# A row of sums spread over partitions: two DMAs through DRAM in the place of a TensorE matmul (two layers of linear attention and MLP)

## The chip, the cores and the metric

The kernel runs on one core of one Trainium2 chip. The metric is the device time of one execution in microseconds (us), lower is better. The engines are called as in the profile: PE (TensorE), DVE (VectorE), ACT (ScalarE), POOL (GpSimd) and SP (SyncE), which here only issues DMAs. POOL issues the large weight loads between its own operations.

## The reference

```python
def A(x, wqkv, wo):                      # linear attention, H = 32 heads of 16
    q, k, v = split(x @ wqkv)            # per head
    phi = lambda t: where(t > 0, t + 1, exp(t)) + 1e-6
    pq, pk = phi(q), phi(k)
    kv = einsum("bhsd,bhse->bhde", pk, v)
    z = einsum("bhsd->bhd", pk)          # the row of phi(K) sums, 512 numbers
    num = einsum("bhqd,bhde->bhqe", pq, kv)
    den = einsum("bhqd,bhd->bhq", pq, z)[..., None] + 1e-6
    return (num / den) @ wo
def B(x, w1, b1, w2, b2):                # MLP, 512 -> 1792 -> 512
    return gelu(layernorm(x) @ w1 + b1) @ w2 + b2
x = x + A(layernorm(x)); x = x + B(layernorm(x))     # layer one
x = x + A(layernorm(x)); x = x + B(layernorm(x))     # layer two
```

x is [1, 2048, 512]; all inputs and the output are bfloat16. Both layers use the same weights.

## The kernel before

**Tiles.** The 2048 tokens are 16 tiles of 128 (one token to a partition), four tiles to a chunk, so four chunks, 0 to 3. Names end in the layer (0 is layer one, 1 is layer two), then the tile or the chunk, then a part: WO0_8 is layer one, tile 8; Q0_1_2 is layer one, chunk 1, part 2.

**Order.** Nothing is scheduled when it runs. Every operation has a name, and `CONF["ORDER"]` (L345) holds one list of names for each engine, written out in full. A planner (`Scheduler`, L114) steps through these lists with its own costs, hands out buffers and PSUM banks, and `assign_waits` (L283) derives the semaphore waits. On the chip each engine goes through its list strictly in order (`play`, L1306): an operation that waits holds up all that stand behind it. SP's list is the order of its DMA issues. `CONF["WAY"]` says which engine does an operation that can go to two.

**The operations around the change**, in the order of the work:

- stats, aggr (DVE), veps, pow (POOL; pow gives rstd), nmr (POOL), norm (DVE or ACT): a layer norm. normB ends in yb.
- TA, TB, TP (SP): DMA transposes of a 128x512 tile (L793 for TA and TB, L1078 for TP). PT (PE, L806) with tc (ACT, L816) is a transpose by PE instead; PTB0_0 and PTB1_0 are such.
- K (L861), Q (L879 by token, L892 by channel), exp, relu, min, phi: phi of keys and queries. G (L962, L994) sums y by phi(K), KV (L1017) multiplies by wv, kvm masks to the heads, M (L1040) multiplies by wo.
- Z (PE, L943) and zs (DVE, L949, L952): the 512 sums of phi(K), as zs[128, 4], that is with channel k*128+p in partition p, column k. zs0_2 is the last of layer one. zb (L1023) is the same, masked, for the chunks whose denominator PE computes by channel (D, L1086; then ln, rec, pr on ACT and DVE or POOL).
- For the chunks whose denominator is computed by token (chunks 2 and 3 of layer one, 1, 2 and 3 of layer two) the 512 sums are needed as one row, the same in all 128 partitions: **zrow**[128, 512]. dz (DVE, L1028) multiplies the identity by zs, ZR (PE, L1031) multiplies a matrix of ones by dz, and cpz (ACT, L975) copies the bank to zrow.
- pz (phi(Q) times zrow, DVE or POOL, L1062), red, den, rec, pr: the denominator by token. pz0_2_0 is the first reader of zrow in layer one.
- WO (PE, L1110): the attention's output, and RA (DVE, L1115): its residual, which frees WO's bank. Two such banks are held at a time.
- W1 (PE, L1142; W10 in layer one, W11 in layer two) with gelu (ACT, L1148), W2 (PE, L1181; W20 and W21) with RB (DVE): the MLP. W10 of chunk 0 is done in two halves: `W10_0_5_0` reads tiles 0 and 1, `W10_0_5_1` tiles 2 and 3. Each of the 14 groups of a half has four matmuls of 256 columns. b2 adds the bias b2 to x (DVE or POOL, L1127).
- w1_0, w1_1, w2_0, w2_1, wv, wo: loads of the weights, issued by POOL (L683). A reader of w1 or of w2 waits for both halves (`Graph.parts`).

The work of layer one's end of attention and start of MLP lies between 34 and 106 us of the span. WO0_8 is the first WO of chunk 2: it reads what TP0_2_0 has transposed, after pr0_2_0. W20_1_0 is the first reader of w2.

Of the kernel before, what the change touches and what calls it, by code (L numbers as in the profile page):

```python
# [10 lines left out]
P = 128  # L11
S = 2048
D = 512
# [269 lines left out]
def assign_waits(graph, order, sems, dma_sems):  # L283
# [10 lines left out]
    while len(done) < total:  # L294
        moved = False
        for e in ENGINES:
# [247 lines left out]
def build_kernel(nc, A_x, A_wqkv, A_wo, B_x, B_w1, B_b1, B_w2, B_b2, out, conf=None, report=False):  # L544
# [5 lines left out]
    with ExitStack() as es:  # L550
# [37 lines left out]
        eps6 = SB("eps6", [P, 1], FP32)  # L588
        dz = SB("dz", [P, D], BF16)
        zrow = SB("zrow", [P, D], BF16)  # L590
        zacc = SB("zacc", [P, D], FP32)
        rd = SB("rd", [P, 4, H], FP32)
        rr = SB("rr", [P, 4, H], FP32)
        if report:
# [783 lines left out]
```

## Time and profile before

| | |
|---|---|
| median of 3 runs | 325.43 us (325.35 to 325.6) |
| profiled execution | 325.09 us |
| its span | 323.4 us |
| mean granted clock of PE in it | 1.0 |

The profile is that of one execution. Its span runs from the first to the last instruction; the execution's own time is 1.7 us longer. A line of the engines in order of time gives start, length, engine, source line, operation, output<-inputs, shapes and how many were merged (x); the bracket gives the idle time of the engine just before it and what ended it. Busy times of PE include the pipeline behind each matmul, so the distance between two starts says what a matmul costs, not its length. PEld is PE's weight load, which overlaps. Lines of DMA issues give KB and the median us from issue to landing. In the lists of groups by line the first number behind the bar is busy us, the second mean ns of one.

### The profile page before, as it was taken

To read this page: it belongs to the slowest core of one execution; us is meant where nothing else is said; L and a number is where in the kernel's file an instruction comes from. 1 tells how busy PE (TensorE), PEld (TensorE's weight loads), DVE (VectorE), ACT (ScalarE), POOL (GpSimd) and SP (SyncE) were. 2 spreads that over 40 slices of the span, in tenths; PEclk is the share of its full clock that TensorE was granted. 3 is DMA by queue.
4 is the path that set the end of the run, shared out by engine and by line. 5 is a ranking of instruction groups with operands and counts; after the bars stand their busy time and mean duration, and the time that the engine had idled before them with its cause. 6 is when DMAs were issued, how large, how long until landed. Compare 5 with 4: busy or idle time off the path is not lost.

```text
span 323.4 us, 4794 instructions
## 1 busy us (share of the span) xinstructions
PE 319.9 (99%) x1725; PEld 159.1 (49%) x1725; DVE 215.5 (67%) x506; ACT 195.1 (60%) x335; POOL 135.4 (42%) x224
## 2 busy tenths in 40 slices
PE   8999999999999999999999999999999999999996
PEld 4444545675444444444444444458644444444443
DVE  5998769999985660214759999999898664000232
ACT  5999698873136129488974657879913734576000
POOL 4672278638703359000366645873902934000000
PEclk9999999999999999999999999999999999999999
DMA  7514458212320105310003200121252243000004
GB/s 246 175 39 94 146 144 305 60 34 59 72 49 12 39 16 99 67 32 2 0 0 68 49 16 2 23 59 36 50 84 49 49 53 79 16 0 2 32 25 155
DMA packets 47572, 20.52 MB, mean 63 GB/s; under 512 B 42620, under 2 KB 46076, under 8 KB 47548
## 3 DMA queue, kind: packets, MB, share of 16 engines
q1 hardware_dynamic: 46076, 15.19, 20.9%
q0 software_dynamic: 1056, 4.72, 4.6%
q10 hardware_dynamic: 416, 0.30, 0.3%
q8 instruction: 14, 0.23, 0.3%
q14 instruction: 10, 0.08, 0.1%
HBM read 8.00 MB, written 2.10 MB: 31 GB/s over the span
## 4 chain that ended last, share of the span: by engine, by line
PE 92%; DVE 6%; POOL 1%; issue 0%
PE ps L1142 30%; PE ps L1181 29%; PE ps L861 9%; PE ps L1110 7%; PE ps L962 4%; PE ps L892 3%; PE ps L879 3%; PE ps L994 2%; PE ps L699 1%; PE ps L1168 1%; DVE gtb L1007 1%; DVE rd L1065 1%; PE ps L943 1%; DVE xsb L1115 1%; DVE gacc L1004 1%; PE ps L1086 1%
## 5 line engine op out<-in xcount | busy, mean ns | idle before, releaser
L1148 ACT ACTIVATE gT<-ps,b1c 128x512 bf16<-128x512 f32 (+1 forms) x140 | 77.2, 600 | 64.4 <-PE ps L1142 63.5
L1142 PE MATMUL ps<-t,w 128*128 128x512 bf16 (+1 forms) x560 | 101.3, 337 | 0.0
L1181 PE MATMUL ps<-w,gT 128*128 128x512 bf16 x434 | 98.4, 379 | 0.0
L1142 PEld LDWEIGHTS ps<-t,w 128*128 128x128 bf16 x560 | 54.5, 98 | 43.8 <-ACT t L816 0.3
L1181 PEld LDWEIGHTS ps<-w,gT 128*128 128x128 bf16 x434 | 42.3, 98 | 50.2
L758 POOL TENSOR_TENSOR rstd<-veps,neghalf 128x1 f32<-128x1 f32 x64 | 39.3, 627 | 5.0 <-DVE veps L756 2.8
L831 ACT ACTIVATE eb<-ps 128x512 bf16<-128x512 f32 x56 | 32.4, 605 | 11.3 <-PE ps L879 3.7
L1191 DVE TENSOR_TENSOR pkb<-ps,xsb 128x512 bf16<-128x512 f32 x15 | 10.2, 685 | 41.5 <-PE ps L1181 41.5
L743 DVE BATCH_NORM_STATS2 stats<-xsb 128x6 f32<-128x512 f32 x48 | 32.1, 677 | 0.3
L861 PE MATMUL ps<-wqkv,t 128*128 128x512 bf16 x128 | 31.4, 379 | 0.0
L1110 PE MATMUL ps<-gtb,t 128*128 128x512 bf16 x128 | 31.3, 380 | 0.1
L842 ACT ACTIVATE rb<-ps 128x512 bf16<-128x512 f32 x38 | 22.8, 607 | 9.3 <-PE ps L861 7.0
L748 POOL TENSOR_SCALAR veps<-mv 128x1 f32<-128x1 f32 x32 | 9.0, 282 | 42.9 <-DVE mv L745 40.9
L756 POOL TENSOR_SCALAR veps<-mv 128x1 f32<-128x1 f32 x28 | 7.1, 258 | 45.5 <-DVE mv L745 44.1
L778 ACT ACTIVATE yb<-xsb,nmr,rstd 128x512 bf16<-128x512 f32 x21 | 16.7, 812 | 11.4 <-POOL nmr L775 11.4
L783 DVE TENSOR_SCALAR yb<-xsb,mv,rstd 128x512 bf16<-128x512 f32 x27 | 14.9, 560 | 11.9 <-POOL rstd L758 11.6
L1187 DVE TENSOR_TENSOR xsb<-ps,xsb 128x512 f32<-128x512 f32 x16 | 10.9, 682 | 16.8 <-PE ps L1181 16.8
L879 PE MATMUL ps<-wqkv,t 128*128 128x512 bf16 x80 | 20.2, 379 | 0.0
L1110 PEld LDWEIGHTS ps<-gtb,t 128*128 128x128 bf16 x128 | 12.3, 98 | 14.8 <-ACT gtb L975 0.3
L861 PEld LDWEIGHTS ps<-wqkv,t 128*128 128x128 bf16 x128 | 12.3, 98 | 14.8 <-ACT t L816 0.3
L844 DVE TENSOR_SCALAR eb<-eb 128x512 bf16<-128x512 bf16 x46 | 13.8, 312 | 8.2 <-ACT eb L831 8.0
L1127 POOL TENSOR_TENSOR xsb<-xsb,b2b 128x512 f32<-128x512 f32 x14 | 17.1, 1218 | 1.0 <-DVE yb L783 0.7
(103 smaller groups left out, 395.0 us busy)
## 6 DMA issues: line engine op xcount, KB each, us to landing
w<-in_B_w_dram POOLq DMA_DIRECT2D x4, 896.0 KB, 7.5
out_dram<-pkb SPq DMA_DIRECT2D x15, 128.0 KB, 2.0
t<-in_A_x_dram SPq DMA_DIRECT2D x3, 512.0 KB, 6.7
t<-yb SPq DMA_TRANSPOSE x57, 2.5
wqkv<-in_A_wqkv_dram SPq DMA_DIRECT2D x1, 512.0 KB, 5.2
wqkv<-in_A_wqkv_dram POOLq DMA_DIRECT2D x1, 512.0 KB, 4.3
wo<-in_A_wo_dram POOLq DMA_DIRECT2D x1, 512.0 KB, 5.7
t<-t SPq DMA_TRANSPOSE x20, 2.5
```

Of the source, the lines that this page charges most:

```text
L743: G.op("dve", lambda e: e.bn_stats(stats[:, s.slot, :], src()), 602, reads=src_keys, writes=[k + "s"], tiles=[s, *src_tiles], prio=prio, n ...
L758: G.op("pool", lambda e: e.tensor_tensor(rstd[:, s.slot:s.slot + 1], veps[:, s.slot:s.slot + 1], neghalf[:], op=ALU.pow), 530, reads=[k + ...
L778: G.op("act", lambda e: e.activation(yb[:, y.slot, :], src(), ACT.Identity, bias=nmr[:, s.slot:s.slot + 1], scale=rstd[:, s.slot:s.slot + 1]),
L831: G.op("act", lambda e: e.activation(eb[:, et.slot, :], bank(bt), ACT.Exp, scale=factor()), 569 if by else 483, reads=[src_key, *more], wr ...
L842: G.op("act", lambda e: e.activation(rb[:, rt.slot, :], bank(bt), ACT.Relu, scale=factor()), 569 if by else 478, reads=[src_key, *more], w ...
L861: ins = e.matmul(bank(b), lhsT=yTa(yT)[:, dt, k * P:(k + 1) * P], rhs=wqkv[:, dt, D:2 * D], start=(dt == 0), stop=(dt == DT - 1))
L879: ins = e.matmul(bank(b), lhsT=yTa(yT)[:, dt, k * P:(k + 1) * P], rhs=wqkv[:, dt, 0:D], start=(dt == 0), stop=(dt == DT - 1))
L1110: ins = e.matmul(bank(wb), lhsT=yTa(pq)[:, kt, k * P:(k + 1) * P], rhs=gtb[:, kt, :], start=(kt == 0), stop=(kt == DT - 1))
L1127: G.op("pool" if on_pool else "dve", lambda e: e.tensor_tensor(xsb[:, st, :], xsb[:, st, :], b2b[:], op=ALU.add), 1120 if on_pool else 600 ...
L1142: ins = e.matmul(bank(b, n), lhsT=w1[:, dt, ft * P:(ft + 1) * P], rhs=yTa(yT)[:, dt, k0 * P:k1 * P], start=(dt == 0), stop=(dt == DT - 1))
L1148: G.op("act", lambda e, ft=ft, b=b, k0=k0, k1=k1, n=n: e.activation(gT[:, g.slot, ft * 512 + k0 * P:ft * 512 + k1 * P], bank(b, n), ACT.Ge ...
L1181: ins = e.matmul(bank(b), lhsT=gT[:, g.slot, ft * 512 + k * P:ft * 512 + (k + 1) * P], rhs=w2[:, ft, :], start=(ft == 0), stop=(ft == FT - 1))
```

## The change

In layer one zrow is made by two DMAs: zsc0 (DVE) copies zs to bfloat16, ZW0 (SP) writes the 128x4 numbers to a DRAM tensor of 512 in the order of channels, and ZB0 (SP) reads these 512 as one row into all 128 partitions. Layer two keeps dz, ZR and cpz.

```diff
+        zsb = SB("zsb", [P, DT], BF16)
+        zscr = nc.dram_tensor("zscr", [D], BF16, kind="Internal").ap()
...
             if any(by_token(L, c) for c in range(NC)):
-                zr = Tile(psum, f"zr{L}", "t")
...
+                if L == 0:
+                    G.op("dve", lambda e: e.tensor_scalar(zsb[:], zs[:], 1.0, None, op0=ALU.mult), 90, reads=["zs"], writes=["zsb"], prio=prio + 8,
+                         name=f"zsc{L}", lat=40)
+                    dma("sp", lambda e: e.dma_start(zscr.rearrange("(k p) -> p k", p=P), zsb[:], allow_slow_non_contiguous=True), ["zscr"], reads=["zsb"], prio=prio + 8, name=f"ZW{L}", kb=2)
+                    dma("sp", lambda e: e.dma_start(zrow[:], bass.AP(zscr.tensor, zscr.offset, [[0, P], [1, D]])), ["zrow"], reads=["zscr"], prio=prio + 8,
+                        name=f"ZB{L}", kb=128)
+                else:
+                    zr = Tile(psum, f"zr{L}", "t")
...
```

The lines behind `else` are those of before (dz, ZR, cpz; L1027 to L1033), indented.

The lists are new in two places. In layer one, from about Z0_2 to the end of W10 of chunk 0 (the parts that differ, cut):

```diff
 PE
-Z0_1 G0_4_0 Z0_2 Q0_1_2 Q0_1_1 G0_5_0 D0_0_3 D0_0_0 G0_6_0 D0_0_1 G0_7_0 D0_0_2 G0_8_0 ZR0 G0_9_0
+Z0_1 G0_4_0 Q0_1_2 Z0_2 Q0_1_1 G0_5_0 D0_0_0 D0_0_1 G0_6_0 G0_7_0 D0_0_2 D0_0_3 G0_8_0 G0_9_0
...
-WO0_8_0 W10_0_3_1 W10_0_12_1 W20_1_0 W10_0_5_1 W10_0_2_1 W20_1_7
+WO0_8_0 W10_0_12_0 W20_1_0 W10_0_10_1 W10_0_12_1 W20_1_7
 DVE
-zs0_1 minq0_1_3 zs0_2 zb0 phiq0_1_3 phiq0_0_1 dz0 minq0_1_0 minq0_1_2 phiq0_1_0 pr0_0_0 minq0_1_1
+minq0_1_0 phik0_9 phiq0_1_0 zs0_1 zs0_2 zsc0 zb0 minq0_1_3 phiq0_0_1 minq0_1_2 phiq0_1_3 minq0_1_1 pr0_0_0
...
-pz0_2_0 red0_2_0 RA0_0 statsB0_0 RA0_1 statsB0_1 aggrB0_0 aggrB0_1 RA0_2 RA0_3 normB0_1 statsB0_2 normB0_0
+pz0_2_0 red0_2_0 RA0_0 statsB0_0 RA0_1 aggrB0_0 statsB0_1 aggrB0_1 den0_2_0 RA0_3 rec0_2_0 normB0_1 RA0_2 normB0_0
+RA0_6 statsB0_2 RA0_4 statsB0_3 aggrB0_3 statsB0_6 pr0_2_0
 POOL
-phik0_6 w1_1 phiq0_1_2 wv wo w2_1 phiq0_1_1 w1_0 pr0_0_2 pr0_1_0 pr0_1_1 w2_0 pr0_1_2 pr0_1_3
+phik0_6 w1_1 w1_0 phiq0_1_1 wv wo phiq0_1_2 pr0_0_2 pr0_1_0 w2_0 pr0_1_1 pr0_1_2 pr0_1_3
...
-b20_0 vepsB0_2 powB0_2 vepsB0_3 powB0_3 phiq0_2_3 pz0_2_1
+b20_0 w2_1 vepsB0_3 powB0_3 vepsB0_2 powB0_2 phiq0_2_3 vepsB0_4
 SP
-Tb1 TB0_1 TB0_2 TB0_3 TP0_2_0 TB0_5
+Tb1 ZW0 ZB0 TB0_1 TP0_2_0 TB0_3 TB0_2 TB0_5
```

In PE's list before, 19 groups of W10 stood between WO0_7 and WO0_8: the 14 of the first half and 5 of the second. In the new one there are 13, all of the first half. In layer two's first chunk the lists of DVE, ACT, POOL and SP are permuted, PE's is not:

```diff
 DVE
-RA1_0 statsB1_0 RA1_1 aggrB1_0 statsB1_1 den1_1_3 aggrB1_1
+RA1_0 RA1_1 statsB1_0 statsB1_1 den1_1_3 aggrB1_1
...
-pr1_1_3 RA1_2 phiq1_3_0 statsB1_2 normB1_0 aggrB1_2 RA1_5 RA1_3
+pr1_1_3 RA1_2 aggrB1_0 statsB1_2 RA1_5 aggrB1_2 normB1_0 phiq1_3_0 RA1_3
```

More of the change, by code (lines that the diff above doesn't have):

```diff
@@ L1026, in attn_kv @@
             if any(by_token(L, c) for c in range(NC)):
-                zr = Tile(psum, f"zr{L}", "t")
-                G.op("dve", lambda e: e.tensor_tensor(dz[:].rearrange("p (k c) -> p k c", k=DT), idp[:].unsqueeze(1).broadcast_to([P, DT, P]),
-                                                      zs[:].unsqueeze(2).broadcast_to([P, DT, P]), op=ALU.mult), 600,
-                     reads=["zs", f"id{P}"], writes=["dz"], prio=prio + 8, name=f"dz{L}", lat=40, fast=True)
-                G.op("pe", lambda e: e.matmul(bank(zr), lhsT=onesm[:, 0:P], rhs=dz[:], start=True, stop=True), MM,
-                     reads=["dz", "onesm"], writes=[f"zr{L}"], tiles=[zr], prio=prio + 8, name=f"ZR{L}", lat=MM_DRAIN)
-                copy(zrow[:], zr, f"zr{L}", "zrow", True, prio + 8, f"z{L}")
+                if L == 0:
[6 more added lines that the diff above has]
+                    zr = Tile(psum, f"zr{L}", "t")
+                    G.op("dve", lambda e: e.tensor_tensor(dz[:].rearrange("p (k c) -> p k c", k=DT), idp[:].unsqueeze(1).broadcast_to([P, DT, P]),
+                                                          zs[:].unsqueeze(2).broadcast_to([P, DT, P]), op=ALU.mult), 600,
+                         reads=["zs", f"id{P}"], writes=["dz"], prio=prio + 8, name=f"dz{L}", lat=40, fast=True)
+                    G.op("pe", lambda e: e.matmul(bank(zr), lhsT=onesm[:, 0:P], rhs=dz[:], start=True, stop=True), MM,
+                         reads=["dz", "onesm"], writes=[f"zr{L}"], tiles=[zr], prio=prio + 8, name=f"ZR{L}", lat=MM_DRAIN)
+                    copy(zrow[:], zr, f"zr{L}", "zrow", True, prio + 8, f"z{L}")
             for kt in range(DT):
```

164 rows, old and new, of the table ORDER are left out of this document.

## The prediction

> **What bounds the kernel now.** I read the page first, then the busy time by stretches, then the engines in order of time where the change lies.
>
> ```profile
> span 323.4 us, 4794 instructions
> PE 319.9 (99%) x1725; PEld 159.1 (49%) x1725; DVE 215.5 (67%) x506; ACT 195.1 (60%) x335; POOL 135.4 (42%) x224
> ```
>
> ```profile
> core 0: us, PE busy (x) PEld busy (x) DVE busy (x) ACT busy (x) POOL busy (x), PEclk, DMA share, GB/s
> 34.00:62.00 28.00, 28.00 (x180) 14.10 (x178) 23.72 (x55) 22.64 (x41) 18.34 (x21) 1.00 0.58 180
> 62.00:106.00 44.00, 44.00 (x257) 24.72 (x255) 38.88 (x85) 21.54 (x46) 20.03 (x30) 1.00 0.22 46
> ```
>
> The page's first part gives TensorE 319.9 of 323.4 us. In the stretch where the edited code runs (34 to 62 us) it is busy 28.00 of 28.00 us, and in the next one 44.00 of 44.00, at granted clock 1.00. A busy share can hide a slow TensorE, so I look at the distance between starts:
>
> ```profile
> 44.83 0.38 PE L1031 MATMUL ps<-dz,onesm 128*128 128x512 bf16 x1
> 45.05 2.32 PE L962 MATMUL ps<-pkb,yb 128*128 128x512 bf16 x10
> ```
>
> The matmul to be removed starts at 44.83 and the next at 45.05. The row says 0.38 us, but a matmul of 512 columns occupies the engine for 0.22; the other 0.16 is pipeline that the next one overlaps. TensorE is thus the bound from end to end: what leaves it is gained whole, what leaves another engine is gained not at all, and a wait on it, however short, is lost. One wait is there already, in layer two:
>
> ```profile
> 212.09 1.03 PE L1110 MATMUL ps<-gtb,t 128*128 128x512 bf16 x4
> 213.06 0.19 POOL L748 TENSOR_SCALAR veps<-mv 128x1 f32<-128x1 f32 x1
> 213.34 0.55 POOL L758 TENSOR_TENSOR rstd<-veps,neghalf 128x1 f32<-128x1 f32 x1
> 213.92 0.55 DVE L783 TENSOR_SCALAR yb<-xsb,mv,rstd 128x512 bf16<-128x512 f32 x1 [0.47 <-POOL rstd L758]
> 214.47 1.25 DVE L1115 TENSOR_TENSOR xsb<-ps,xsb 128x512 f32<-128x512 f32 x2
> 214.68 0.39 PE L806 MATMUL ps<-idp,yb 128*128 128x128 bf16 x4
> 215.18 1.41 PEld L1110 LDWEIGHTS ps<-gtb,t 128*128 128x128 bf16 x8 [0.30 <-DVE xsb L1115]
> 215.19 1.90 PE L1110 MATMUL ps<-gtb,t 128*128 128x512 bf16 x8
> ```
>
> VectorE waits 0.47 us for GpSimd's rstd at normB1_0 (213.92). Behind it in VectorE's list stands RA1_5, the first of the two at 214.47, and WO1_7 (215.19) needs the bank that RA1_5 frees. The bracket shows the weight load idle 0.30 us for L1115; the four matmuls at 214.68 take 0.39 - 0.16 = 0.23 us, so matmuls could go on at 214.91 and go on at 215.19: 0.28 us lost.
>
> **The change part by part.** *TensorE:* ZR0 goes, -0.22 us. No matmul is added; the rest are permuted.
>
> *ScalarE and VectorE:*
>
> ```profile
> L1028 DVE TENSOR_TENSOR dz<-idp,zs 128x512 bf16<-128x512 bf16 x2 | 1.4, 682 | 0.0
> L975 ACT ACTIVATE zrow<-ps 128x512 bf16<-128x512 f32 x2 | 1.2, 592 | 0.7 <-PE ps L1031 0.7
> L935 DVE TENSOR_SCALAR zs<-ps 128x4 f32<-128x4 f32 x1 | 0.2, 151 | 0.0
> ```
>
> ScalarE loses cpz0, 0.59 us. VectorE loses dz0 (0.68) and gains zsc0, a copy of 128x4 for which L935 is the nearest row, 0.15. Both savings lie beside a TensorE without a gap, so I count them as nothing; they only widen margins.
>
> *The two DMAs.* The trace has no write of 512 two-byte elements. The nearest rows:
>
> ```profile
> t<-yb SPq DMA_TRANSPOSE x57, 2.5
> out_dram<-pkb SPq DMA_DIRECT2D x15, 128.0 KB, 2.0
> t<-in_A_x_dram SPq DMA_DIRECT2D x2, 128.0 KB, 2.6
> b2b<-in_B_b_dram SPq DMA_DIRECT2D x1, 128.0 KB, 3.3
> b1t<-b1r SPq DMA_TRANSPOSE x1, 7.3
> w<-in_B_w_dram POOLq DMA_DIRECT2D x1, 896.0 KB, 7.6
> wqkv<-in_A_wqkv_dram POOLq DMA_DIRECT2D x1, 512.0 KB, 4.3
> wo<-in_A_wo_dram POOLq DMA_DIRECT2D x1, 512.0 KB, 5.7
> w<-in_B_w_dram POOLq DMA_DIRECT2D x1, 896.0 KB, 5.8
> ```
>
> The last number is us from issue to landing. The row of 7.6 is w1_1, issued beside b2b and b1t; the row of 5.8 is w2_0, the last load. b1t moves 4 KB and still took 7.3 us, as long as the load beside it. So ZW0 costs between 2.0 (a store to DRAM) and 7.3 (beside a load), ZB0 between 2.6 and 7.3. When do they start, and beside what?
>
> ```profile
> 35.20 0.94 POOL L683 DMA_DIRECT2D w<-in_B_w_dram  x1
> 38.39 0.54 PE L943 MATMUL ps<-onesm,pkb 128*128 128x1 bf16 x16
> 38.97 0.16 DVE L952 TENSOR_TENSOR zs<-ps,zs 128x4 f32<-128x4 f32 x1 [0.61 <-PE ps L943]
> 52.24 0.68 DVE L1062 TENSOR_TENSOR lr<-t,zrow 128x512 f32<-128x512 bf16 x1
> 58.30 6.67 SPq L793 DMA_TRANSPOSE t<-yb  x3
> ```
>
> w1_1 is issued at 35.20 and takes GpSimd 0.94; the new list puts w1_0 right behind it, at 36.1, so ZW0 runs beside that load. Z0_2 (38.39) moves behind one group of four 512-column matmuls, 0.86 us, so zs0_2 comes at 39.85 and zsc0 ends at 40.2. The first reader of zrow is pz0_2_0 (52.24), due at 52.0 without ZR0. The chain lands between 40.2 + 2.0 + 2.6 = 44.8 and 40.2 + 7.3 + 7.3 = 54.8. I take 49.4: ZW0 until w1_0 is in (36.1 + 7.6 = 43.7), then ZB0 beside wv and wo, as long as wo took, 5.7. That is 2.6 us early: cost 0, behind the matmuls of G0, KV0 and M0. SP's next instruction behind them, TB0_1, went at 58.30, so its in-order wait holds up nobody.
>
> The Trainium skill, "DMA: Bandwidth & Descriptors", section "Rules for kernel authors", speaks against the form: a last dimension that is not contiguous is lowered to one descriptor per element, here 512 for 1 KB. No run here shows this. The nearest row, a DMA transpose, lands in 2.5 us; the sum by either is the same, since 12 us are free.
>
> *The loads moved on GpSimd.* wv now waits behind phiq0_1_1:
>
> ```profile
> 42.98 0.79 POOL L683 DMA_DIRECT2D wqkv<-in_A_wqkv_dram  x1
> 59.41 1.16 POOL L1127 TENSOR_TENSOR xsb<-xsb,b2b 128x512 f32<-128x512 f32 x1 [0.72 <-DVE yb L783]
> 48.72 0.39 PE L1017 MATMUL ps<-gtb,wqkv 128*128 128x128 bf16 x4
> 50.91 0.81 PE L1040 MATMUL ps<-wo,kvb 128*128 128x512 bf16 x3
> ```
>
> phiq0_1_1 needs minq0_1_1, which I place at 42.3, and lasts 1.2 (as b20_0 at 59.41, also a 128x512 operation of GpSimd), so wv goes at 43.5 instead of 42.98 and wo 0.8 later, at 44.3. wv lands at 43.5 + 4.3 = 47.8, due 48.5 (KV0_0, 48.72 - 0.22); wo at 44.3 + 5.7 = 50.0, due 50.7. Hidden, with 0.7 us each.
>
> w2_1 moves furthest, from behind wo to behind b20_0.
>
> ```profile
> 60.18 0.60 ACT L816 ACTIVATE t<-ps 128x512 bf16<-128x512 bf16 x1 [0.75 <-PE ps L806]
> 60.85 8.38 PE L1142 MATMUL ps<-t,w 128*128 128x256 bf16 x75
> 65.42 0.68 DVE L1074 TENSOR_TENSOR t<-t,rr 128x512 bf16<-128x512 bf16 x1
> 66.14 1.20 SPq L1078 DMA_TRANSPOSE t<-t  x1
> ```
>
> b20_0 ended at 59.41 + 1.16 = 60.57; normB0_0 ahead of it comes about 0.35 earlier in the new list, so w2_1 is issued at 60.2. Its reader is W20_1_0, which waits for both halves of w2. The new list puts 13 groups W10 ahead of WO0_8; a group of four 256-column matmuls takes 0.44 (8.38 us for 19 groups, one record missing). From 60.63 that makes WO0_8 due at 66.3, and W20_1_0, behind WO0_8 (0.86) and one more group, at 67.6. Bounds for w2_1 are 5.8 and 7.6: 66.0 to 67.8. I take 5.8, since like w2_0 it has no other load starting beside it: 66.0, hidden by 1.6 us.
>
> But TP0_2_0, which WO0_8 waits for, now runs beside w2_1. pr0_2_0 comes forward from 65.42 to about 62.0 (I counted the entries ahead of it at 0.6 us per 512-wide operation), so TP0_2_0 is issued at 62.7. Alone it lands at 65.2; if it ends only with the load, as b1t did, at 66.0; due 66.3. I take 66.0: no wait, with 0.3 us to spare. TB0_3 and TB0_2 follow at about 64.0 and 65.4 and land by 67.9; the second half of W10, which needs them, now starts behind W20_1_0 at 69.1.
>
> *The other permutations of layer one* swap near neighbours. The one that moves an input of TensorE is zb0: it ends at about 40.9 now, and its reader, the first D0, stands behind Z0_2 (39.25, 0.38) and two groups of four (1.73), so at 41.4. No wait; if these margins are misjudged, it is a wait of tenths, which the range covers.
>
> *Layer two's lists.* TensorE's order stays. RA1_5 now stands ahead of normB1_0. WO1_5 (212.09, ends 213.12) releases it; it runs to 213.85, inside the 0.47 us in which VectorE waited for rstd. aggrB1_0 moves behind RA1_2 (about 212.6), still ahead of its reader at 213.06. So the 0.28 us go, the transposes at 214.68 stay on time, and next in line is WO1_6, with RA1_3 0.3 us earlier too. Bounds: 0 to -0.28; I take -0.28.
>
> *Sum:* -0.22 - 0.28 = -0.50 us. The profiled execution took 325.09 us with its span of 323.4, and is 0.34 below the median of the runs, 325.43; taken off the median, **324.9 us**.
>
> **The rivals.** *B, loads and transposes collide, slower.* The mechanism is w2_1 behind b20_0: if it takes w1_1's 7.6 us, it lands at 67.8, TP0_2_0 with it, and WO0_8 waits 67.8 - 66.3 = 1.5 us: 324.9 + 1.5 = 326.4. At 7.0 us it is 0.9, 325.8. It is slower than before from a landing at 66.8 on. For it: b1t and w1_1 landed together. Against it: w2_0 took 5.8. Beside this, the Trainium skill, "DMA: Bandwidth & Descriptors", section "Queues, rings and completion order", says that a semaphore increment is a strongly ordered write that lands after every earlier write of its DMA engine, across queues. By that rule, TP0_2_0 lands no earlier than what w2_1 has queued ahead of it; the row of b1t agrees (7.3 beside 7.6).
>
> *C, zrow late.* At both upper bounds, 54.8 against 52.0, pz0_2_0 stalls VectorE for 2.8 us; behind it stand RA0_0, the statistics and norms of chunk 0, and then all of W10, whose first group started at 60.85, 0.07 after tcB0_0 (60.18 + 0.60) had written its input: 324.9 + 2.8 = 327.7. It decides from a landing after 52.0. Against it: it takes 7.3 us twice, where w1_0 should be in by 43.7.
>
> *D, layer two's wait stays* (normB1_0 late by as much as RA1_5 is early, or another bank): 325.43 - 0.22 = 325.2.
>
> *E, the change doesn't act:* if ZR0 were no part of the bound, 325.4; the 0.22 us between the two starts speak against it.
>
> **How the numbers follow.** Forecast 324.9 (own range 324.6 to 325.1): 0.50. B, from a wait of 0.3 to one of 1.5 us, 325.2 to 326.4: 0.25. C: 0.10. D: 0.12. E: 0.03. Below 324.6 I leave 0.03 and above 326.4 C and a little of B, 0.12; so the range is 324.6 to 326.4. 0.2% is 0.65 us, about what a measurement of this kernel can tell from no change: faster is under 324.78, slower over 326.08. The forecast lies 0.14 above the first of these, so I give faster 0.08, out of the forecast's lower edge. Slower gets all of C and 0.10 of B, 0.20. The rest, 0.72, is the same.
>
> **What would show it.** Right: a span of about 322.9; one L1031 matmul instead of two; L1110's weight loads without the idle time for L1115 near 215; VectorE without a gap ahead of pz0_2_0, ZB0 landed by about 49.4. Wrong: a gap on TensorE ahead of WO0_8 near 66 or W20_1_0 near 67.6 with w2_1 or TP0_2_0 landing there (B); VectorE idle near 52 for a DMA (C); a gap ahead of KV0_0 near 48.5 (wv late); the gap near 215 unchanged (D). A new gap anywhere else would be one that I haven't seen.

## The result and the profile after

The changed kernel takes 340.97 us (median of 5 runs, 338.51 to 341.49) against 325.54 of the kernel before beside it (325.35 to 325.6): a ratio of 1.0464, 95% interval 1.0441 to 1.0486. It is 15.4 us slower where 0.5 us faster was forecast, far outside the range of 324.6 to 326.4. The profiled execution took 341.49 us. One execution of the kernel before and one of the version with three DMAs (below) ran at a granted clock of 0.66 from end to end and took 483.8 and 485.26 us; they count in none of the numbers here.

The page of the changed kernel, its first two parts (busy time, then tenths in 40 slices of 8.5 us):

```profile
span 339.6 us, 4761 instructions
...
PE 320.1 (94%) x1693; PEld 159.9 (47%) x1724; DVE 218.9 (64%) x506; ACT 195.2 (57%) x334; POOL 135.0 (40%) x224
...
PE   8999980699999999999999999999999999999996
...
PEclk9999996599999999999999999999999999999999
```

TensorE has as much work as before (319.9 then, 320.1 now) in a span that is 16.2 us longer. The seventh slice, from 51 us on, is empty, and in that slice and the next the granted clock is 0.6 and 0.5. Its longest wait, and its work in order of time there (the bracket: idle time just before, and what ended it):

```profile
PE ps L1019 <- DMA wqkv<-in_A_wqkv_dram: 13.2, 1, 13.2
```

```profile
48.87 0.38 PE L964 MATMUL ps<-pkb,yb 128*128 128x512 bf16 x1
62.43 0.59 PE L1019 MATMUL ps<-gtb,wqkv 128*128 128x128 bf16 x4 [13.18 <-DMA wqkv<-in_A_wqkv_dram]
...
66.66 1.20 PE L1049 MATMUL ps<-wo,kvb 128*128 128x512 bf16 x4
```

It is KV0_0 (L1019) that waits for wv. The matmul at 48.87 occupies 0.22, so TensorE stood for 62.43 - 49.09 = 13.34 us. Then it is slow. From KV0_0 to the first M0 (L1049) it needed 48.72 to 50.91 = 2.19 us before (rows of the prediction) and 62.43 to 66.66 = 4.23 now, 2.04 more (0.2 of it comes with the new lists: without ZW0, below, the same stretch takes 49.03 to 51.43, 2.40). The busy time by stretches says why, in its column PEclk:

```profile
49.00:62.50 13.50, 0.32 (x4) 0.10 (x3) 2.22 (x4) 1.44 (x3) 3.07 (x3) 0.66 0.63 66
62.50:67.00 4.50, 4.28 (x22) 2.62 (x24) 1.48 (x5) 1.93 (x4) 1.15 (x1) 0.50 0.68 229
67.00:106.00 39.00, 38.24 (x234) 22.67 (x237) 37.46 (x78) 20.93 (x43) 23.92 (x31) 1.00 0.34 65
```

After the wait the clock is 0.50 for some 4 us, then 1.00 again. The Trainium skill, "TensorE: Matmul & The Clock Gate", "Part 1: The HAM clock gate", gives a warm-up of about 3.4 us at half rate after idling; this trace agrees, with some 4 us.

Why did wv come so late? The DMA issues between 38 and 62 us (last number: us from issue to landing):

```profile
w<-in_B_w_dram POOLq DMA_DIRECT2D x1, 896.0 KB, 15.5
wqkv<-in_A_wqkv_dram POOLq DMA_DIRECT2D x1, 512.0 KB, 18.2
wo<-in_A_wo_dram POOLq DMA_DIRECT2D x1, 512.0 KB, 19.1
zrow<-zscr SPq DMA_DIRECT2D x1, 128.0 KB, 8.0
zscr<-zsb SPq DMA_DIRECT2D x1, 1.0 KB, 18.0
```

ZW0 (zscr), 1 KB, takes 18.0 us, and each load issued beside it 15 to 19 where 4.3 to 5.8 were shown before. w1_0, issued just ahead of it, took 18.3 (w1_1 and w1_0 have a median of 12.8, and w1_1 took 7.3). Between 49 and 59 us the loads' queue, q0, shows this after and before (packets, MB, the time that they took as a share of 16 engines):

```profile
q0 software_dynamic: 80, 0.30, 61.3%
```

```profile
q0 software_dynamic: 586, 2.59, 71.8%
```

After, 80 packets took 0.613 x 16 x 10 us = 98 us of engine time, 1.2 us each on average (single ones up to 12); before, 586 packets took 115 us, 0.2 each. The engines are taken up by the loads' packets, but they move a ninth of the bytes. ZW0's own packets, in SP's queue q1, aren't among them: 474 packets of q1 stand between 43 and 44 us and none between 46 and 58.

Two places that the prediction named remain. WO0_8 waits for TP0_2_0 (weight loads of TensorE, and the DMAs from 76 to 85 us: w2_1 and TP0_2_0):

```profile
PEld ps L1119 <- DMA t<-t: 0.7, 1, 0.7
```

```profile
w<-in_B_w_dram POOLq DMA_DIRECT2D x1, 896.0 KB, 6.2
...
t<-t SPq DMA_TRANSPOSE x1, 4.0
```

And in layer two the wait ahead of WO1_7 is gone:

```profile
231.15 0.39 PE L808 MATMUL ps<-idp,yb 128*128 128x128 bf16 x4
231.37 0.81 PE L1119 MATMUL ps<-gtb,t 128*128 128x512 bf16 x3
```

From 231.15 to 231.37 are the 0.22 that four such matmuls need; before, 214.68 to 215.19.

Of the 0.7 us for TP0_2_0 TensorE itself loses about 0.5: its 52 matmuls of W10 start from 76.76 on at 0.11 from one another, so that it is free at 82.48, and the weight load starts at 83.01. The account: 13.34 + 2.04 + 0.5 - 0.50 (ZR0 and the wait of layer two) = 15.4, as between the medians. The two profiled spans differ by 16.2; 0.7 of that lies ahead of the change (w1_1 was issued at 35.92 instead of 35.20), which differs between executions (last section).

### The profile page after: what moved, and what is told of

Its sections match the earlier page's. It is cut to its first block, busy times and chain, and to the rows that moved or that the text cites. A ratio compares the mean times of both kernels' runs of the same rounds, so it can differ in the third digit from the quotient of the medians.

```text
span 339.6 us, 4761 instructions
## 1 busy us (share of the span) xinstructions
PE 320.1 (94%) x1693; PEld 159.9 (47%) x1724; DVE 218.9 (64%) x506; ACT 195.2 (57%) x334; POOL 135.0 (40%) x224
## 4 chain that ended last, share of the span: by engine, by line
PE 86%; DMA 7%; DVE 4%; POOL 1%; issue 1%; SPq 0%; POOLq 0%
PE ps L1190 27%; PE ps L1151 27%; PE ps L863 8%; DMA wqkv<-in_A_wqkv_dram 7%; PE ps L1119 6%; PE ps L881 5%; PE ps L996 4%; PE ps L894 3%; PE ps L964 2%; DVE xsb L1124 1%; DVE stats L745 1%; PE ps L1177 1%; PE ps L1019 1%; PE ps L945 1%; PE ps L1049 1%
## 5 line engine op out<-in xcount | busy, mean ns | idle before, releaser
L1190 PE MATMUL ps<-w,gT 128*128 128x512 bf16 x424 | 97.4, 379 | 0.5
L750 POOL TENSOR_SCALAR veps<-mv 128x1 f32<-128x1 f32 x32 | 8.2, 257 | 44.8 <-DVE mv L747 42.9
L758 POOL TENSOR_SCALAR veps<-mv 128x1 f32<-128x1 f32 x28 | 7.2, 261 | 45.1 <-DVE mv L747 43.7
L1103 POOL TENSOR_TENSOR t<-t,lr 128x512 bf16<-128x512 bf16 x9 | 10.5, 1167 | 20.2 <-ACT lr L1099 20.0
```

Of the source, the lines that this page charges most:

```text
L1190: ins = e.matmul(bank(b), lhsT=gT[:, g.slot, ft * 512 + k * P:ft * 512 + (k + 1) * P], rhs=w2[:, ft, :], start=(ft == 0), stop=(ft == FT - 1))
```

## The experiments

All times are medians beside the kernel before on the same chip (325.4 to 325.6 there). The theories: **S**, writes that lie close together in DRAM wait for each other, and hold up the loads' packets; **W**, any small write to DRAM is slow; **D**, the number of descriptors is what costs; **L**, the loads' new order is to blame, not ZW0. Some expectations use a letter otherwise and say so: in the first kernel below L is that ZW0 was slow only because of the loads beside it; in the runs without ZW0 and with the lists of before W is that ZW0 holds up the loads.

**The write by itself, in four layouts.** The kernel before with writes of the same 1 KB, whose data nothing uses, set in three stretches without loads; two kernels, one execution each.

```diff
+ dma("sp", ... zscr.rearrange("(k p) -> p k", p=P), zsb[:] ...)         # PW1: 512 x 2 B, dense, as ZW0; then PB1, the broadcast
+ dma("sp", ... zrun.rearrange("(p k) -> p k", p=P), zsb[:])             # PW2: 128 runs of 8 B, dense
+ dma("sp", ... zpad[:, 0].rearrange("(k p) -> p k", p=P), zsb[:] ...)   # PW3: 512 x 2 B, 512 B apart
```

> The kernel before, with DMAs added in stretches in which SP and the weight loads are idle; nothing waits for them, and their data are a constant. PW1, behind TA1_7 (about 141 us): the 512 two-byte writes of ZW0, alone. PB1 behind it: the row read into 128 partitions. PW2, behind TA1_14 (about 186 us): the same 512 numbers as 128 runs of 8 bytes. PW3, behind TB1_11 (about 275 us): 512 two-byte writes, each 512 bytes from the next. Theory W (small writes to DRAM are slow by themselves): PW1 lands after 15 to 18 us with no load beside it; PW2, a quarter of the writes, after 4 to 6 us. Theory L (ZW0 was slow only because of the loads beside it): PW1 lands in 2 to 3 us, PW2 and PW3 too. Theory S (writes into the same lines of DRAM wait for each other): PW1 is slow as under W, but PW3 lands in 2 to 4 us. Time of the kernel as before, 325.5 +- 0.5, in all cases, if SP is free again before its next transposes (207 and 303 us).

It took 325.7 us. Its writes in the three stretches:

```profile
zscr<-zsb SPq DMA_DIRECT2D x1, 1.0 KB, 14.0
```

```profile
zrun<-zsb SPq DMA_DIRECT2D x1, 1.0 KB, 3.4
```

```profile
zpad<-zsb SPq DMA_DIRECT2D x1, 1.0 KB, 2.3
```

The second kernel: a DMA transpose and a store of four rows of 256 B in the place of the dense write (TZ1, PW5, PB5), 512 x 2 B at 64 B from one another (PW4, zp), and 512 x 2 B into SBUF (PW6, zb).

> The kernel before, with DMAs added in the same stretches. TZ1, PW5, PB5 (about 141 us): a DMA transpose of 128x128, a store of four rows of 256 bytes to DRAM, and the row read into 128 partitions, each waiting for the one ahead. PW4 (about 186 us): 512 two-byte writes to DRAM, 64 bytes from each other. PW6 (about 275 us): 512 two-byte writes into SBUF instead of DRAM. Theory W: PW6 lands in 2 to 4 us, since it doesn't write to DRAM; PW4 as slow as the dense form, 15 to 18 us. Theory S (same lines): PW4 lands in 2 to 5 us. Theory D (the number of descriptors counts, not the target): PW6 takes as long as the dense form to DRAM. The chain: 2.5 + 2 + 2.6 = 7 us under all of them, since it has no two-byte write.

It took 325.22 us. The issues, stretch by stretch; for PW5 SP's own times, since PB5 waits for its landing:

```profile
zrow<-zscr SPq DMA_DIRECT2D x1, 128.0 KB, 2.9
...
zT<-zt SPq DMA_TRANSPOSE x1, 2.4
```

```profile
143.93 0.28 SPq L1294 DMA_DIRECT2D zscr<-zT  x1
145.10 0.35 SPq L1295 DMA_DIRECT2D zrow<-zscr  x1
```

```profile
zp<-zsb SPq DMA_DIRECT2D x1, 1.0 KB, 2.0
```

```profile
zb<-zsb SPq DMA_DIRECT2D x1, 1.0 KB, 2.2
```

ZW0's write takes 14.0 us with no load beside it. The same 512 elements take 2.0 as soon as they stand 64 B apart, and 2.2 in SBUF; four rows take 1.2. D falls (the number of writes is the same in 14.0 and 2.0), W falls, and S stands: if the writes wait one after the other, it is (14.0 - 2.0) / 512 = 23 ns for each that has neighbours, an estimate.

Where they wait shows in the first kernel's queue of SP, from 143.0 to 143.5 us:

```profile
q1 hardware_dynamic: 527, 0.00, 50.2%
```

The write was issued at 142.02. All its 512 packets pass the DMA engines in this half microsecond (the other 15 have 4 B); between 144 and 156 us q1 has none, and the write lands at 156.0. So the descriptors cost the engines little, and the 12 us are spent behind them. In the changed kernel, too, ZW0's packets are through by 46 us and it lands at 58.8: the loads' packets are slow meanwhile. That the writes wait for each other in the memory is the reading that fits both; no trace shows the memory itself.

Beside this, the Trainium skill, "DMA: Bandwidth & Descriptors", "Rules for kernel authors", warns of this form because of one descriptor per element; the warning is borne out here, its reason isn't: the one descriptor per element is there, but 512 elements 64 B apart cost no more than a store (2.0).

**ZW0 left out.** The changed kernel without ZW0; ZB0 waits for zsc0 instead and reads a row of b2, so zrow isn't the row of sums.

> The changed kernel without ZW0: the sums are not written to DRAM, and ZB0 fills zrow with the row b2 instead, so the denominators by token of layer one are other numbers. All lists stay as changed. Theory W (ZW0 holds up the loads): wv lands at about 48, KV0_0 doesn't wait, and the time falls from 341.0 to 325.0 to 326.3; what is left above 324.9 is a wait of WO0_8 for TP0_2_0 beside w2_1 (0.8 us in the changed kernel's trace). Theory L (the new order of the loads makes wv late, with ZW0 as its victim): wv still lands near 62, and the time stays above 338.

326.0 us, ratio 1.0016 (1.0006 to 1.0027). Its load of wv, and TensorE's one wait for a DMA from 38 to 90:

```profile
wqkv<-in_A_wqkv_dram POOLq DMA_DIRECT2D x1, 512.0 KB, 4.3
```

```profile
PE ps L1118 <- DMA t<-t: 0.4, 1, 0.4
```

So 15 of the 15.4 us are ZW0's. What is left, 0.6, is still slower than before, and WO0_8's wait for TP0_2_0 is in it.

**The DMAs with the lists of before.** dz0, ZR0 and cpz0 out, zsc0, ZW0 and ZB0 in, every other name where it stood.

> The kernel before with the two DMAs in the place of dz0, ZR0 and cpz0, and with all lists as before otherwise (wv issued at 43.0, w1_0 behind w2_1). Theory W: ZW0 is issued at 39.2, and wv and wo, issued behind it, land 10 us and more late: 335 to 342. Theory L: the order of the loads of before keeps wv in time, and ZW0 lands in a quiet stretch: 325.0 to 325.6.

341.61 us, 1.0501 (1.0473 to 1.0529). DMA issues and TensorE's waits:

```profile
wqkv<-in_A_wqkv_dram POOLq DMA_DIRECT2D x1, 512.0 KB, 17.5
...
zscr<-zsb SPq DMA_DIRECT2D x1, 1.0 KB, 17.5
```

```profile
PE ps L1019 <- DMA wqkv<-in_A_wqkv_dram: 11.6, 1, 11.6
PE ps L1119 <- DVE xsb L1124: 2.7, 4, 0.9
```

L falls: the loss is there in the old order too. Its second line, four waits for RA, is taken up below.

**The writes 64 B apart, in place.** The changed kernel, with

```diff
-zscr = nc.dram_tensor("zscr", [D], ...)
+zscr = nc.dram_tensor("zscr", [D, 32], ...)
```

and ZW0 writing column 0.

> The changed kernel in place, with one thing other: ZW0's 512 two-byte writes stand 64 bytes apart in DRAM (ZB0 waits for them as before, but broadcasts a row of b2 instead of what was written, so the output isn't the reference's). Theory S: ZW0 lands within 2 to 5 us, no load is held, and the time is that of the kernel without ZW0, 326.0 (325.7 to 326.5). Rival D (the 512 descriptors beside loads are what costs, not the lines that they share): ZW0 takes over 10 us, wv lands after 55, 333 to 341.

325.88 us, 1.0015 (1.0005 to 1.0024). Its DMA issues:

```profile
wqkv<-in_A_wqkv_dram POOLq DMA_DIRECT2D x1, 512.0 KB, 4.5
...
zrow<-in_B_b_dram SPq DMA_DIRECT2D x1, 128.0 KB, 4.6
...
zscr<-zsb SPq DMA_DIRECT2D x1, 1.0 KB, 4.9
```

ZW0, ZB0 and all their descriptors are there beside the loads, and the 15 us are gone. That settles the cause: it is the distance of the writes, not their number, nor DMAs beside loads. (64 B apart they also spread over 32 KB instead of one; the runs don't tell these two apart.)

**The lists alone.** The changed kernel's lists with dz0, ZR0 and cpz0 in the place of zsc0, ZW0 and ZB0.

> The lists alone: the changed kernel's order on every engine, the row still spread by TensorE (dz0, ZR0, cpz0 put back). Theory S (the 512 writes that share lines of DRAM hold the queues; the lists are a small thing beside it): the kernel without ZW0 took 326.0; with ZR0 back 0.2 more, so 326.2 (326.0 to 326.5), wv, w2_1 and the loads between land within 4 to 7 us of their issue, and TensorE waits 0.5 us at WO0_8 for TP0_2_0, as there. Rival L (part of the loss is the lists', and showed only together with the DMAs): over 328.

325.65 us, 1.0009 (0.9999 to 1.0018), less than expected. TensorE's weight loads waited for VectorE's copies ahead of KV0, and only 0.2 us for TP0_2_0: WO0_8's weight load started at 67.41, and at 67.67 without ZW0. The first of these:

```profile
PEld ps L1019 <- DVE gtb L980: 0.9, 2, 0.6
```

But for ZR0, dz0 and cpz0 here, and zsc0 and ZB0 there, this kernel and the one without ZW0 have the same lists, so the two show what ZR0 is worth in them. First without ZR0, then with it (the line of PEld is a weight load of WO):

```profile
47.16 0.38 PE L1094 MATMUL ps<-t,zb 128*128 128x512 bf16 x1
...
59.68 0.55 PEld L1118 LDWEIGHTS ps<-gtb,t 128*128 128x128 bf16 x4 [0.58 <-DVE xsb L1123]
60.56 0.39 PE L808 MATMUL ps<-idp,yb 128*128 128x128 bf16 x4
```

```profile
47.36 0.38 PE L1095 MATMUL ps<-t,zb 128*128 128x512 bf16 x1
...
59.60 0.61 PEld L1119 LDWEIGHTS ps<-gtb,t 128*128 128x128 bf16 x4 [0.26 <-DVE xsb L1124]
60.54 0.39 PE L808 MATMUL ps<-idp,yb 128*128 128x128 bf16 x4
```

TensorE is level ahead of ZR0 (44.35 and 44.34), without it 0.20 ahead behind it, and level again at 60.5. In between a weight load of WO waits for VectorE's RA, which starts at 58.95 without ZR0 and at 58.87 with it. So in the change's lists VectorE takes back what ZR0 gave: the 0.22 is won on TensorE and not in the time.

**Layer two's lists alone**, layer one as before.

> Layer two's lists alone, everything else as before. If the prediction's term for layer two holds (RA1_5 ahead of normB1_0, the weight load no longer waits for L1115): 0.28 us less than before, 325.1 to 325.2, and no gap on TensorE near 215. Rival D (the wait stays or moves to another bank): as before, 325.4, with a gap of about 0.3 us near 215 or just behind it.

325.25 us, 0.9995 (0.9986 to 1.0004). The median gives less than the 0.28, and its interval, -0.46 to +0.13 us, takes in both; the trace shows the step itself:

```profile
214.64 0.39 PE L806 MATMUL ps<-idp,yb 128*128 128x128 bf16 x4
214.86 1.46 PE L1110 MATMUL ps<-gtb,t 128*128 128x512 bf16 x6
```

214.64 to 214.86: no wait is left, and its span is 323.0 against 323.4. Lists alone minus this one is what layer one's new lists cost, about 0.4 us (each of the two medians is good to some 0.3).

**A mend: three DMAs.** Layer one's lists of before, layer two's new ones, and the row by DMAs that don't write side by side:

```diff
+zt, zT = SB("zt", [P, P], BF16), SB("zT", [P, P], BF16)    # zt zeroed; zsc0 writes zt[:, 0:4]
+TZ0: dma_start_transpose(zT, zt);  ZW0: zscr.rearrange("(k p) -> k p", p=P) <- zT[0:4, :];  ZB0 as in the change
```

> A version that could beat both: layer one's order as before, layer two's as changed, ZR0, dz0 and cpz0 gone, and the row spread by three DMAs whose writes don't share a line: the sums into a 128x128 tile, a DMA transpose, four rows of 256 bytes to DRAM, the broadcast. Theory S: the chain took 6.4 us alone; beside the loads up to twice that, so zrow lands at 47 to 53 against 52 that it is due; no load is held (wv within 4.3 to 5 us), and the time is 325.4 - 0.22 - 0.28 = 324.9 (324.7 to 325.3). Rival T (a transpose or a small store beside a load ends only with the load): the chain of three lands at 55 or later, and VectorE's pz0_2_0 waits: 326 to 329. Rival W (any small store to DRAM holds the queues): 335 or more.

327.55 us (four executions of 327.38 to 327.66), 1.0065 (1.0051 to 1.0079). The expectation of 324.9 did not hold. Next, the same version with its profile, and **a mend with two DMAs**: the DMAs with layer one's lists of before, layer two's new ones, and ZW0 in another layout:

```diff
-zscr.rearrange("(k p) -> p k", p=P), zsb[:]
+zscr.rearrange("(p k) -> p k", p=P), zsb[:]               # 128 runs of 8 B
-tensor_tensor(lr[:, r.slot, :], tok(), zrow[:])
+tensor_tensor(lr "b (k p) -> b k p", tok() "b (k p) -> b k p", zrow "b (p k) -> b k p")   # layer one
```

> The version with three DMAs again, for its profile: it took 327.4 to 327.7, against 324.9 expected, and its profile there was at a clock of 0.66 from end to end. Rival R: TZ0, ZW0 and ZB0 each end only with the load beside them, zrow lands at 54 to 54.5 with w1_0, VectorE's pz0_2_0 waits some 2 us for it, and TensorE stands as long ahead of the first W10 group near 61. Theory W (the small store holds the loads): wv lands over 6 us after its issue and TensorE waits at KV0_0 near 48.5. Otherwise: a gap elsewhere, which would be a third cause.

> Two DMAs as in the change, but ZW0 writes 128 runs of 8 bytes (a partition's four sums side by side) and pz0's read zrow with a step of 8 bytes; layer one's order as before with dz0, ZR0 and cpz0 gone, layer two's as changed. Theory S: 128 writes of this form took 3.4 us alone; beside w1_1 ZW0 lands at 43 to 46, ZB0 beside wv and wo by 47 to 51, before the 52.0 at which zrow is due; no load over 8 us; 325.4 - 0.22 - 0.28 = 324.9 (324.7 to 325.2). Rival R (zrow late: ZB0 ends with w2_1 or w1_0 at 52 to 54.4, as is suspected of the version with three DMAs): 325.5 to 327.5. Rival W (any small store into one KB beside loads holds the queues): over 330.

327.93 us (1.0078, 1.006 to 1.0095) and 328.42 us (1.009, 1.0073 to 1.0107). Neither S nor R nor W names the cause; what the first expectation left over, a gap elsewhere, came. In the version with three DMAs, first the DMA that fills zrow, then TensorE's only line of waits between 38 and 90 us:

```profile
zrow<-zscr SPq DMA_DIRECT2D x1, 128.0 KB, 5.3
```

```profile
PE ps L1122 <- DVE xsb L1127: 1.6, 3, 0.8
```

TZ0 was issued at 40.4 and zrow in at 50.1, in time, so R falls. The waits are for VectorE's RA, though VectorE isn't late: the first RA starts 1.07 us after the first WO, as before. TensorE stands where it didn't stand before. In the version with two DMAs:

```profile
55.05 1.89 PE L1121 MATMUL ps<-gtb,t 128*128 128x512 bf16 x8
57.11 1.04 PE L1121 MATMUL ps<-gtb,t 128*128 128x512 bf16 x4 [0.16 <-DVE xsb L1126]
...
58.93 1.90 PE L1121 MATMUL ps<-gtb,t 128*128 128x512 bf16 x8
61.63 1.04 PE L1121 MATMUL ps<-gtb,t 128*128 128x512 bf16 x4 [0.80 <-DVE xsb L1126]
```

Twelve matmuls in a row have become eight, a wait, and four, twice. By the distance of starts TensorE loses 0.33 and 0.97 us at these two and 0.85 at the next WO, 2.15 in all. A third cause suggests itself: the planner hands PSUM banks out as it walks through the lists, and ZR0 held one, bank 6. Without it, KV0 gets bank 4, Q0_2_2 that bank after it, and WO0_1 to WO0_6 turn in two banks (5 and 3) instead of three (3, 5 and 4), so that each third one waits for an RA that has only begun. (These numbers are the planner's, and its own plan has WO0_7 at 62.5 us instead of 60.3; the trace names no banks.)

**The bank held.** The same version, and

```diff
+zr = Tile(psum, "zr0", "t")
+for o in G.ops:
+    if o.name in ("G0_9_0", "reluq0_1_1"): o.tiles.append(zr); zr.users += 1
```

> The version with runs of 8 bytes, and one thing other: the bank that ZR0 held stays held as long (by G0_9_0 until reluq0_1_1), so that every later matmul of both layers gets the bank that it has in the version of layer two's lists alone. Theory K (without ZR0 the builder hands the banks out anew: WO0_1 to WO0_6 turn in two banks, 5 and 3, where they turned in three, and each third one waits for VectorE's RA0): the waits for L1126 of 0.32, 0.96, 0.85 and 0.21 us between 56 and 75 are gone, and the time is 325.4 - 0.22 - 0.28 and up to 0.4 for wo, which lands late beside ZB0: 325.0 to 325.4. Rival (wo landing at 52, 0.25 to 0.4 us late, pushes the rest behind it): the waits stay, 327.5 to 328.5.

325.06 us (324.7 to 327.4), ratio 1.000 (0.9985 to 1.0016) where it was 1.009 without the hold. TensorE has no wait for RA left, and the twelve are in a row again:

```profile
53.87 2.75 PE L1121 MATMUL ps<-gtb,t 128*128 128x512 bf16 x12
```

So are the next twelve, at 57.32. With the bank held, the planner gives every matmul the bank that it has with layer two's lists alone (G0_9_0 holds the extra one besides), so the banks are the cause of these waits. Here ZR0's time is won and kept: against that kernel TensorE is 0.41 us behind at Z0_2 (38.76, 38.35) and 0.20 behind at PTB0_0 (59.91, 59.71).

The median is 0.49 below that of the kernel before beside it, 325.55, which is what the prediction's sum of -0.50 says of the two steps that are left. But two of its twelve executions took over 327 us, at a granted clock of 0.997 where the others have 0.999 or 1.0; why is open, and with them the interval can't tell it from the kernel before. No version here beats the kernel before measurably.

**Two loads moved as well:** w1_0 behind w1_1, w2_1 behind phiq0_1_1.

> The same, with two loads of GpSimd's list changed as well: w1_0 right behind w1_1, w2_1 behind phiq0_1_1, so that w2_1 no longer runs beside ZB0, wv and wo. Theory K and S together: wo lands by 50.5, nothing waits, 325.4 - 0.22 - 0.28 = 324.9 (324.7 to 325.2). Rival: ZW0 beside w1_0 lands at 45.5 and ZB0 then beside wo at 50.2, and either wo (due 50.7) or zrow (due 52.0) is late by tenths: 325.2 to 325.8.

327.18 us, 1.0044 (1.0031 to 1.0057). Its load of wv, and TensorE's wait:

```profile
wqkv<-in_A_wqkv_dram POOLq DMA_DIRECT2D x1, 512.0 KB, 6.8
```

```profile
PE ps L1019 <- DMA wqkv<-in_A_wqkv_dram: 1.0, 1, 1.0
```

The rival's cause is there, on wv instead of wo: with w1_0 beside it ZW0 took 7.1 us (4.4 in the version before), and wv came 1.0 us past its time. The two loads alone don't do that: in the same order of the loads up to wo, with ZW0's writes 64 B apart (above), ZW0 took 4.9 and wv 4.5. The rival's range, 325.2 to 325.8, was missed. About 1 us of the 2.1 between the last two medians isn't explained; in the profiled execution the work was 0.85 us later from its start on (w1_1 issued at 36.55 and at 35.70).

## Why the prediction was wrong

- **The step that failed** is "So ZW0 costs between 2.0 (a store to DRAM) and 7.3 (beside a load)", and what was built on it: "cost 0". ZW0 costs 14.0 us alone and 18.0 here. The bounds came from rows of transfers that write whole rows; none writes 512 neighbours of two bytes. The prediction named this gap ("The trace has no write of 512 two-byte elements") and then filled it with those rows as if they were ends.
- **The second half of the same failure**: a slow ZW0 was priced only through its reader (rival C, zrow late at 52.0). zrow did come late, issued at 58.9 and landed 8.0 us later, but TensorE was standing by then. The loss went through wv, whose packets slowed down beside ZW0: "Hidden, with 0.7 us each" holds without ZW0 (4.3 us in the run without it, no wait for wv) and fails by 13 us with it.
- **Not priced at all:** the clock. 13 us of standing still cost some 2 more afterwards.
- **TensorE as the bound** was right for what was lost: it stands as waits on TensorE and in its clock. "From end to end" was too much: in the change's lists, between WO0_0 and PTB0_0, VectorE's RA is so close behind that it takes back 0.2 us won on TensorE.
- **ZR0, -0.22**: right in size (0.20 and 0.21 on TensorE, in the change's lists and with the bank held), but "what leaves it is gained whole" fails twice. In the change's own lists, seen without ZW0, RA takes it back by 60.5. And ZR0 also held a bank: taken out of the old order, it costs 2.9 us by the ratios of the version with two DMAs without and with the hold, 1.009 and 1.000, of which 2.15 stand in its trace as the three gaps.
- **Rival B** was real, but small: TP0_2_0 landed with w2_1, and WO0_8's weight load stood 0.4 us without ZW0 and 0.7 in the changed kernel, where 0.3 to 1.5 was given and the forecast had no wait. The mechanism, TP0_2_0 beside w2_1, was right, but without a slow load: w2_1 took 5.9 us without ZW0, where 5.8 was forecast, and TP0_2_0 landed some 0.4 us behind it.
- **The other permutations of layer one**, "a wait of tenths": so it is, the lists alone wait for VectorE's copies ahead of KV0.
- **Layer two, -0.28**: right by the traces; the gap is gone in the trace after and in the trace of that list alone. The medians don't tell it from no gain.
- **The Trainium skill's rule** on non-contiguous elements was weighed, and put aside with "the sum by either is the same, since 12 us are free". Its direction was right. A price for it could not be had from the trace; the range should then have been open upwards.

## What to carry to other kernels

Before a DMA with elements of a few bytes goes to DRAM, look at how far apart they land: side by side they cost 14 us for 1 KB, 64 B apart 2. Price such a DMA by the loads that run beside it, not only by its reader. And where buffers are handed out by a planner, an operation taken out can move every bank behind it: compare the banks before counting its time as won, and look whether the next engine is close behind.

## What the runs showed that was not expected

- 512 writes of 2 B into 1 KB of DRAM: 14.0 us; 128 of 8 B into the same KB: 3.4; 512 of 2 B at 64 B: 2.0, at 512 B: 2.3; into SBUF: 2.2. The distance at which it ends lies between 2 and 64 B; where, and which unit makes them wait, wasn't measured. The DMA engines are through with the 512 packets in the first 2 us of the 14.0.
- Until such a write lands, packets of loads take 1.2 us on average instead of 0.2.
- zrow read by VectorE with a step of 8 B costs nothing: 0.68 us for 128x512, as before.
- The first matmuls of the span start at times that differ by 1 us and more between profiled executions: w1_1 was issued at 35.20 in the trace before, at 36.13 in the first kernel with the write by itself, whose lists up to there are the same, and at 36.55 in the last version.
